# Block products of the output projection of batches 2 and 3: seven for eight

## The chip, the cores and the metric

The kernel runs on 1 core of one Trainium2 chip. The metric is the device time of one execution in microseconds (us); lower is better. The engines are TensorE (PE, matrix products into PSUM), VectorE (DVE), ScalarE (ACT), GpSimd (POOL) and SyncE (SP, which issues the DMAs).

## What is computed

```python
# attention: q, k, v of (4, 12, 448, 64), causal, float32
scores = np.where(mask, -1e9, (1 / np.sqrt(64)) * np.matmul(q, k.transpose(0, 1, 3, 2)))
attn = np.exp(scores - max); attn = attn / (sum + 1e-09)
attn_out = np.matmul(attn, v)
# tokens (1792 = 4 batches x 448) times weights (768 x 768), float32
x = attn_out.transpose(0, 2, 1, 3).reshape(1792, 768)
h = np.maximum(np.maximum(x @ w1, x @ w2), x @ w3)
out = h @ w_out
```

## The kernel before

Float32 values are split into two float16 planes, a high and a low one, so that one float32 product of a 128 x 128 weight block with a 128 x 448 token block is three matmuls on PE (high-high, high-low, low-high), each 448 columns wide. Everything is kept transposed: blocks of 128 features on the partitions, the 448 tokens of a batch along the free dimension. `w16[j]` holds the planes of w1, w2, w3 (j = 0 to 2) and of the output weights (j = 3).

Attention runs batch by batch (`staging`, `attend`), head pairs in turn, and fills x, whose low half is written on DVE (L532). For batches 0 and 1, `hidden` (L1022) makes six hidden blocks of 3 x 18 matmuls each, and `project` (L1315) the output: for each of six column blocks of the output weights 6 row blocks x 3 = 18 matmuls into one PSUM bank, an eviction with a scale (L512 on ACT, L514 on DVE) into `osb`, and a store (L1329, SP).

The hidden products of batches 2 and 3 are done together, by `seven` (L1246): x of the two batches, cut in two by features, is one 2 x 2 block matrix, w1 to w3 cut in two both ways is another, and seven products of combined blocks stand for the eight plain ones. For each of i = 0 to 2 (a 128-wide slice of both column halves) and j = 0 to 2 (the weight matrix), seven products of 9 matmuls each are summed up in five PSUM banks and folded together on DVE (L1259: read PSUM, scale, add; one fold after another in the same buffers e1, u3, c22). The maximum over j is taken on DVE (L1290), and the four hidden blocks of i are split in planes (high half L512 on ACT or L514 on DVE, low half L532 on DVE).

The combined operands are made ahead of it: `weights_combined` (groups S) rebuilds four float32 weight blocks from their planes (`load`, L1100, on DVE or POOL; a first sum at L1149), combines them (L1105, DVE) and splits four results in planes (high half L512 or L514, low half L532, 128 x 384), 16 instructions for each of the nine (i, j). `tokens_combined` (groups T) does the same for x (sums at L1179). All but the first S read `DONE`, that is, they wait until x of batch 3 is complete, since their buffers lie where attention's were. `columns` makes the per-column scale factors.

`project` of batches 2 and 3 takes the hidden blocks in pairs (z, z + 3), the pairs of the later i last, so that matmuls on the first hidden blocks can run while the last are being made.

The order of all work is written out: `ORDER` lists every instruction group in the order of issue over all engines, `ENGINE` names its engine. A POOL instruction is made to wait for the DVE instruction last ordered ahead of it that works from SBUF (`port=True`). PSUM has 8 banks; in this stage the ring M has 3 and L has 5. SBUF regions are used twice, first for attention and then for the late stage (`regions`). The kernel's matmuls of the late stage all have the same form:

```python
for wl, hl in ((0, 0), (0, 1), (1, 0)):
    PE.matmul(T(M)[:, 0:S_LEN], w16[3][:, f, wl, es], T(("h", b, f))[:, hl], start=..., stop=...)
```

## Time and profile before

| | |
|---|---|
| time, median of 3 runs | 468.86 us (468.77 to 470.32) |
| the profiled execution, its own time | 471.05 us |
| its span, first to last instruction | 469.3 us |
| PE busy | 460.2 us (98%), 3732 matmuls |
| DVE busy | 390.6 us (83%) |
| ACT busy | 309.3 us (66%) |
| POOL busy | 137.7 us (29%) |
| mean granted clock of PE | 0.996 of full speed |

Times in the rows are us from the start of the span unless marked ns. A group's row gives line, engine, operation, output <- input, shapes and count, then its busy time, the mean of one, and the idle time of the engine just ahead of them. L12 is line 12 of the kernel; a helper's line stands for all its callers.

### The profile page before, as it was taken

The numbers are of one execution on the slowest core, as the hardware profiler recorded it, in microseconds if no ns is written. First come the engines' busy times: TensorE is split into PE (matmuls) and PEld (weight loads), VectorE is DVE, ScalarE is ACT, GpSimd is POOL, SyncE is SP. The second block draws the span as 40 slices with busy tenths as digits, with TensorE's granted clock in tenths as the row PEclk, the third lists the DMA queues.
The fourth block names the chain that finished last, engine by engine and source line by source line (L and its number), as shares of the span: only waits on it lengthen the run. The fifth ranks groups of instructions, "written<-read, shape, count | busy, mean of one in ns | idle before, by whom it ended". The sixth has DMA issues, their size and how long they took to land.

```text
span 469.3 us, 9754 instructions
## 1 busy us (share of the span) xinstructions
PE 460.2 (98%) x3732; PEld 269.5 (57%) x3732; DVE 390.6 (83%) x750; ACT 309.3 (66%) x730; POOL 137.7 (29%) x164
## 2 busy tenths in 40 slices
PE   7999999999999999999999999999999999999996
PEld 4778765565665556565556556655555555555553
DVE  3899999999999998896568979888999988897510
ACT  4899999999999999876776788783422411211202
POOL 4024523461433334631265442301032130000000
PEclk9899999999999999999999999999999999999999
DMA  8856378998998877656757744762100000000122
GB/s 236 293 176 217 117 233 224 229 211 184 188 225 227 201 234 198 129 102 146 143 124 159 171 87 71 170 123 47 39 0 2 0 1 1 1 0 1 49 91 97
DMA packets 102319, 60.40 MB, mean 129 GB/s; under 512 B 76672, under 2 KB 99712, under 8 KB 102272
## 3 DMA queue, kind: packets, MB, share of 16 engines
q1 hardware_dynamic: 102272, 59.78, 51.2%
q8 instruction: 29, 0.48, 0.4%
q14 instruction: 18, 0.15, 0.1%
HBM read 35.39 MB, written 5.51 MB: 87 GB/s over the span
## 4 chain that ended last, share of the span: by engine, by line
PE 85%; DVE 7%; ACT 3%; DMA 2%; issue 1%; POOL 1%; SPq 1%; ACTq 0%; DVEq 0%; POOLq 0%
PE M L1022 24%; PE M L1315 15%; PE L L1246 12%; PE S L706 11%; PE M L1246 7%; PE O L820 6%; PE O L1246 4%; PE L L1315 2%; DMA region<-in_k_dram 2%; DVE acc L733 1%; DVE region L938 1%; DVE region L930 1%; DVE region L942 1%; ACT region L744 1%; PE M L551 1%
## 5 line engine op out<-in xcount | busy, mean ns | idle before, releaser
L1022 PE MATMUL M<-x,w 128*128 128x448 f16 x648 | 127.9, 353 | 0.2 <-POOL x L523 0.2
L1022 PEld LDWEIGHTS <-w 128*128 128x128 f16 x648 | 61.2, 98 | 58.1 <-issue 3.1
L744 ACT ACTIVATE region<-S,acc 128x384 f32<-128x384 f32 (+3 forms) x168 | 82.3, 503 | 8.5 <-DVE acc L733 5.6
L523 POOL TENSOR_TENSOR region<-region 128x1024 f16<-128x1024 f32 x23 | 49.0, 2132 | 80.9 <-ACT region L512 26.1
L733 DVE TENSOR_REDUCE acc<-S 128x2 f32<-128x512 f32 (+2 forms) x96 | 61.5, 682 | 12.0 <-PE S L706 10.3
L706 PE MATMUL S<-region 64*128 64x384 f32 (+4 forms) x384 | 66.6, 404 | 0.4 <-DMA region<-in_k_dram 0.4
L1315 PEld LDWEIGHTS <-w 128*128 128x128 f16 x432 | 41.4, 98 | 38.1
L1315 PE MATMUL M<-h,w 128*128 128x448 f16 x288 | 56.9, 353 | 0.0
L512 ACT ACTIVATE region<-region,acc 128x256 f32<-128x256 f32 (+3 forms) x94 | 45.4, 533 | 11.5 <-DVE acc L774 11.5
L706 PEld LDWEIGHTS S<-region 64*128 64x128 f32 (+1 forms) x384 | 40.6, 188 | 18.7 <-issue 11.2
L512 ACT ACTIVATE region<-region,cols 128x384 f16<-128x384 f32 (+1 forms) x31 | 18.3, 612 | 47.4 <-DVE region L1105 23.5
L1246 PEld LDWEIGHTS <-region 128*128 128x128 f16 x324 | 31.7, 98 | 29.6
L512 ACT ACTIVATE region<-region 128x1024 f16<-128x1024 f32 (+2 forms) x48 | 40.8, 863 | 9.1 <-DVE region L1179 3.9
L1100 POOL TENSOR_TENSOR region<-w 128x384 f32<-128x384 f16 x16 | 15.3, 968 | 72.8 <-DVE region L1100 27.1
L1246 PE MATMUL L<-region,region 128*128 128x448 f16 x180 | 36.3, 352 | 0.0
L1246 PEld LDWEIGHTS <-w 128*128 128x128 f16 x243 | 23.6, 98 | 22.0
L744 ACT ACTIVATION_READ_ACCUMULATOR region<-S,acc 128x1 f32 x168 | 34.7, 206 | 0.0
L1246 PE MATMUL M<-x,w 128*128 128x448 f16 x162 | 32.8, 353 | 0.0
L820 PEld LDWEIGHTS <-region 128*64 128x64 f16 x1080 | 26.7, 111 | 9.1 <-issue 8.2
L820 PE MATMUL O<-region,region 128*64 128x128 f16 (+1 forms) x1080 | 30.6, 211 | 0.1
L512 ACT ACTIVATE hacc<-M,cols 128x448 f32<-128x448 f32 x9 | 5.7, 631 | 30.5 <-PE M L1246 20.4
L532 DVE SCALAR_TENSOR_TENSOR w<-region,wf,w 128x768 f16<-128x768 f32 x20 | 20.5, 1038 | 4.6 <-POOL w L516 4.3
(152 smaller groups left out, 733.5 us busy)
## 6 DMA issues: line engine op xcount, KB each, us to landing
region<-in_moe_w_dram SPq DMA_DIRECT2D x18, 768.0 KB, 4.4
region<-in_q_dram SPq DMA_DIRECT2D x24, 224.0 KB, 3.4
region<-in_k_dram SPq DMA_DIRECT2D x24, 224.0 KB, 3.4
out_dram<-osb SPq DMA_DIRECT2D x24, 224.0 KB, 2.0
region<-in_v_dram SPq DMA_DIRECT2D x12, 384.0 KB, 5.9
region<-in_moe_w_out_dram SPq DMA_DIRECT2D x6, 768.0 KB, 4.4
region<-in_v_dram SPq DMA_DIRECT2D x4, 192.0 KB, 5.2
region<-region SPq DMA_TRANSPOSE x36, 4.6
```

Source lines behind the costliest of these rows:

```text
L512: ACT.activation(o, i, AF.Copy, scale=f)
L523: ENG[eng].tensor_tensor(out=o, in0=i, in1=hi, op=ALU.subtract)
L532: DVE.scalar_tensor_tensor(out=o, in0=i, scalar=f, in1=hi, op0=ALU.mult, op1=ALU.subtract)
L551: PE.matmul(T(M)[:, i * P : i * P + P], ap(c, 0, [[0, P]]), ident, start=True, stop=True)
L706: PE.matmul(o[:, c : c + w], l, r, start=start, stop=True, skip_group_check=True)
L733: DVE.tensor_reduce(out=T(acc)[:, at : at + len(g)], in_=i, op=ALU.max, axis=AX.XY if parts == 2 else AX.X, negate=True)
L744: ACT.activation(part(T(y), parts, c, w), part(T(S), parts, c, w), AF.Exp, bias=T(acc)[:, at : at + 1], accum_out=T(acc)[:, 7 + at : 8 + at])
L820: PE.matmul(T(O)[D * h : D * h + D, P * i : P * i + w], vt[j][:, vl, (2 * p + h) * D : (2 * p + h + 1) * D], T(pT[u])[:, 8 * pl + c, a : a ...
L1022: PE.matmul(T(M)[:, 0:S_LEN], w16[j][:, kk, wl, fs], xx[:, kk % 3, xl], start=(kk == 0 and wl + xl == 0), stop=(kk == 5 and wl == 1))
L1100: add(c_add(n), lambda e: ENG[e].tensor_tensor(out=o(), in0=a()[0], in1=a()[1], op=ALU.add), reads=reads, writes=writes, ring=ring, prio=p ...
L1246: PE.matmul(T(M)[:, 0:S_LEN], stat(c, wl), mov(c, xl), start=first and n == 0, stop=n == 8, skip_group_check=True)
L1315: PE.matmul(T(M)[:, 0:S_LEN], w16[3][:, f, wl, es], T(("h", b, f))[:, hl], start=(f == 0 and hl + wl == 0), stop=(f == 5 and wl == 1))
```

## The change

`project` is now used for batches 0 and 1 only. For batches 2 and 3, `project_seven` takes the hidden blocks of the two batches as one 2 x 2 block matrix (batch by feature half) and the output weights as another, and forms seven products of 9 matmuls for each of three column pairs, each issued in two parts (row blocks 0 and 1, then 2), in five PSUM banks, with two evictions, five folds on DVE and four stores. `weights_combined` is called for j = 3 too (three more sets of 16 instructions), with constants for scale factors. `heads_combined` makes the combined hidden blocks for each i: a difference, three scaled differences on DVE, and four splits in planes; one of the four plain hidden blocks of each i (12) is no longer split. The new planes have buffers of their own (`uA`, `uB`) in regions that are now used a third time, and in x of batch 3. `h3` shrinks from 6 to 3 buffers. `ORDER` (1865 entries before, 1958 after) and `ENGINE` are new throughout.

```diff
--- before
+++ after
@@ -32,129 +32,135 @@
-ORDER = [16, 15, 17, 18, 19, 20, 30, 21, 31, 32, 48, 49, 50, 0, 2, 3, 4, 1, 6, 5, 47, 22, 23, 24, 26, 27, 25, 28, 29,
...
@@ -167,7 +173,7 @@
...
-    tT=4, tS=6, tL=8, h3=6, Se=2, Sl=6, tE=3, L=5)
+    tT=4, tS=6, tL=8, h3=3, Se=2, Sl=6, tE=3, L=5, uA=2, uB=1)
...
@@ -426,12 +432,12 @@
...
-        Se=([P, DM], F32), Sl=([P, DM], F32))
+        Se=([P, DM], F32), Sl=([P, DM], F32), uA=([P, 3, 2, S_LEN], F16), uB=([P, 3, 2, S_LEN], F16))
-        (("p32", "ph", "pT"), ("Sl", "tS")), (("wst", "w3"), ("tT",)), (("vr",), ("Se", "tE")), (("v16",), ("tL",)),
-        (("qr", "kr"), ("h3",)))
+        (("p32", "ph", "pT"), ("Sl", "tS")), (("wst", "w3"), ("tT",)), (("vr",), ("Se", "tE"), ("uA",)), (("v16",), ("tL",)),
+        (("qr", "kr"), ("h3", "uB")))
...
@@ -496,6 +503,7 @@
+    pc = wmx
@@ -1088,8 +1096,15 @@
...
+        def heads(e):
+            rec(pc[:, 12:15], wg[:, 0:3])
+            tt(out=pc[:, 0:3], in0=wg[:, 3:6], in1=pc[:, 12:15], op=ALU.mult)
+            for k, f in ((3, 0.5), (6, 0.25), (9, -0.25)):
+                times(pc[:, k : k + 3], wg[:, 0:3], f)
+
+        add([("dve", 0.7)], heads, reads=["kap"], writes=["pc"], prio=prio, port=True)
@@ -1117,11 +1132,11 @@
...
-        od.group = f"S{3 * i + j}"
+        od.group = f"S{3 * i + j if j < 3 else 9 + i}"
-        kp, kn = kap[:, q : q + 1], kap[:, 9 + q : 10 + q]
+        kp, kn = (kap[:, q : q + 1], kap[:, 9 + q : 10 + q]) if j < 3 else (1.0, -1.0)
@@ -1140,7 +1155,8 @@
...
-            planes(lambda: at(0), lambda: at(1), lambda: g(name)().rearrange("p (a b) -> p a b", b=P), kpa[:, f + q : f + q + 1],
+            planes(lambda: at(0), lambda: at(1), lambda: g(name)().rearrange("p (a b) -> p a b", b=P),
+                   kpa[:, f + q : f + q + 1] if j < 3 else (0.25 if f else 0.5),
@@ -1248,7 +1264,7 @@
...
-                add([("pe", 9 * c_pe(S_LEN))], mm, reads=reads + (DONE if z != 1 else []), writes=[M], ring=ring, prio=pr + 0.01 * at,
+                add([("pe", 9 * c_pe(S_LEN))], mm, reads=reads + (DONE if z != 1 else []), writes=[M, ("pd", i, j, at)], ring=ring, prio=pr + 0.01 * at,
@@ -1291,7 +1307,7 @@
...
-        for z, b, f in ((11, 2, i), (12, 3, i), (22, 3, i + 3), (21, 2, i + 3)):
+        for z, b, f in ((11, 2, i), (22, 3, i + 3), (21, 2, i + 3)):
@@ -1300,6 +1316,116 @@
...
+
+    UN = [("x", 3, 0), ("uB", 0), ("uA", 0), ("uA", 1)]
+
+    def heads_combined(c, prio):
+
+        od.group = f"T{3 + c}"
+        o = {z: ("tL", "c", c, z) for z in (11, 12, 21, 22)}
+        one_, two = ("tL", "v", c), ("hacc", "v", c)
+        ratio = pc[:, c : c + 1]
+        seen = [(TT[z], k) for z in range(4) for k in range(3)] + [("pd", 0, 0, k) for k in range(7)]
+
+        def less(t, a, b, ring=None, reads=()):
+            add([("dve", c_sb(S_LEN))],
+                lambda e: DVE.scalar_tensor_tensor(
+                    out=T(t), in0=T(a), scalar=ratio, in1=T(b), op0=ALU.mult, op1=ALU.subtract),
+                reads=[a, b, "pc"] + list(reads), writes=[t], ring=ring, prio=prio, port=True)
+
+        def plane(z, t, k):
+            u, f = UN[z], pc[:, k + c : k + c + 1]
+            r = ("uB" if z == 1 else "uA", u) if z and c == 0 else None
+            add([("act", c_act(S_LEN, 0.06)), ("dve", c_dve(S_LEN, True) + 0.06)],
+                lambda e: scaled(e, T(u)[:, c, 0], T(t), f), reads=[t, "pc"] + seen + ([(u, "u", 0, 0)] if c else []),
+                writes=[(u, "u", c, 0)], ring=r, prio=prio, port=True)
+            add([("dve", c_sb(S_LEN))], lambda e: scaled_rest("dve", T(u)[:, c, 1], T(t), f, T(u)[:, c, 0]),
+                reads=[t, (u, "u", c, 0)], writes=[(u, "u", c)], prio=prio, port=True)
+
+        add(c_add(S_LEN), lambda e: ENG[e].tensor_tensor(out=T(one_), in0=T(o[12]), in1=T(o[11]), op=ALU.subtract),
+            reads=[o[12], o[11]], writes=[one_], ring=("tL", one_), prio=prio, port=True)
+        less(two, o[22], one_, ("hacc", two))
+        less(o[12], o[22], o[12])
+        plane(0, one_, 3)
+        plane(1, two, 6)
+        plane(2, o[12], 3)
+        less(o[21], o[21], two, reads=[(("h", 2, c + 3), 1)])
+        plane(3, o[21], 9)
+
+    def project_seven(prio):
+        f4, f16, m4 = (pc[:, 15 + z : 16 + z] for z in range(3))
+        f1 = osc[:, 2:3]
+        for ee in range(3):
+            od.group = f"j{12 + ee}"
+            s = [("Sw", ee, 3, z) for z in range(2)]
+            bank = {z: ("P", 3, ee, z) for z in (1, 4, 5, 6, 7)}
+            e1, u3, c11, c22 = (("tL", n, 3, ee) for n in ("e1", "u3", "c11", "c22"))
+            es = [slice((ee + 3 * z) * P, (ee + 3 * z + 1) * P) for z in range(2)]
+
+            def w(half, z, es=es):
+                return (lambda c, hl: w16[3][:, 3 * half + c, hl, es[z]]), lambda c: [("w", 18 + 3 * half + c)]
+
+            def sw(z, s=s):
+                def at(c, hl):
+                    return T(s[z // 2]).bitcast(F16).rearrange("p (s c h f) -> p s c h f", s=2, c=3, h=2)[:, z % 2, c, hl]
+
+                return at, lambda c: [(s[z // 2], z % 2, 0), (s[z // 2], z % 2)]
+
+            def hb(b, half):
+                return (lambda c, hl: T(("h", b, 3 * half + c))[:, hl]), lambda c: [(("h", b, 3 * half + c), z) for z in range(2)]
+
+            def ub(z):
+                return (lambda c, hl: T(UN[z])[:, c, hl]), lambda c: [(UN[z], "u", c, 0), (UN[z], "u", c)]
+
+            def product(z, stat, mov, first, at, bank=bank):
+                M = bank[z]
+                for part in ((0, 1), (2,)):
+
+                    def mm(e, part=part):
+                        for c in part:
+                            for wl, xl in ((0, 0), (0, 1), (1, 0)):
+                                PE.matmul(
+                                    T(M)[:, 0:S_LEN], stat[0](c, wl), mov[0](c, xl), start=first and c + wl + xl == 0,
+                                    stop=c == 2 and wl == 1, skip_group_check=True)
+
+                    claim = first and part[0] == 0
+                    add([("pe", 3 * len(part) * c_pe(S_LEN))], mm, reads=[n for c in part for n in stat[1](c) + mov[1](c)],
+                        writes=[M], ring=(("M" if z == 1 else "L"), M) if claim else None, prio=prio + 0.2 * ee + 0.01 * at,
+                        chain="L" if claim and z != 1 else None)
+
+            def evict(o, ring, bank=bank):
+                add([("act", c_act(S_LEN, 0.02)), ("dve", c_dve(S_LEN) + 0.06)],
+                    lambda e: scaled(e, T(o), T(bank[1])[:, 0:S_LEN], f1), reads=[bank[1], ("osc", 2)], writes=[o], ring=(ring, o),
+                    prio=EV)
+
+            def fold(o, z, f, a, reads, writes, ring=None, bank=bank):
+                add([("dve", c_dve(S_LEN) + 0.06)],
+                    lambda e: DVE.scalar_tensor_tensor(
+                        out=T(o), in0=T(bank[z])[:, 0:S_LEN], scalar=f, in1=T(a), op0=ALU.mult, op1=ALU.add),
+                    reads=[bank[z], ("osc", 2)] + reads, writes=writes, ring=ring, prio=EV)
+
+            def store(o, z, b, es=es):
+                add(c_dma((P, 4 * S_LEN)), lambda e: ENG[e].dma_start(out[es[z], b * S_LEN : (b + 1) * S_LEN], T(o)), reads=[o],
+                    prio=EV)
+
+            product(1, w(0, 0), hb(2, 0), True, 0)
+            evict(e1, "hacc")
+            product(6, sw(2), ub(1), True, 1)
+            fold(e1, 6, f16, e1, [], [e1])
+            product(1, w(1, 0), hb(2, 1), False, 2)
+            evict(c11, "osb")
+            store(c11, 0, 2)
+            product(7, sw(1), ub(2), True, 3)
+            fold(u3, 7, f4, e1, [e1], [u3], ("tL", u3))
+            product(5, sw(0), ub(0), True, 4)
+            fold(c22, 5, f4, u3, [u3], [c22], ("tL", c22))
+            store(c22, 1, 3)
+            product(4, w(1, 1), ub(3), True, 5)
+            fold(u3, 4, m4, u3, [], [u3])
+            store(u3, 1, 2)
+            product(5, sw(3), hb(3, 1), False, 6)
+            fold(e1, 5, f4, e1, [], [e1])
+            store(e1, 0, 3)
 
     def project(b, prio):
         for e2 in range(KC):
@@ -1345,16 +1471,27 @@
                     if i + j:
                         weights_combined(i, j, 400 + 10 * (3 * i + j))
             for i in range(3):
+                weights_combined(i, 3, 500 + 10 * i)
+            for i in range(3):
                 seven(i, prio + 0.1 + 0.2 * i)
+                heads_combined(i, prio + 0.2 + 0.2 * i)
+        else:
+            return
 
         od.group = "k"
 
         def factor(e):
             DVE.tensor_scalar(
                 out=osc[:, b : b + 1], in0=bsc[:, b, 9:10] if b < 2 else bsc[:, 2, 8:9], scalar1=wu[:, 6:7], scalar2=2.0**18, op0=ALU.mult, op1=ALU.mult)
-
-        add([("dve", 0.13)], factor, reads=[("scale", b) if b < 2 else "beta", "wu"], writes=[("osc", b)], prio=prio)
-        project(b, prio)
+            if b == 2:
+                for z, f in enumerate((4.0, 16.0, -4.0)):
+                    DVE.tensor_scalar(out=pc[:, 15 + z : 16 + z], in0=osc[:, 2:3], scalar1=f, scalar2=None, op0=ALU.mult)
+
+        add([("dve", 0.13 if b < 2 else 0.5)], factor, reads=[("scale", b) if b < 2 else "beta", "wu"], writes=[("osc", b)], prio=prio)
+        if b < 2:
+            project(b, prio)
+        else:
+            project_seven(prio + 1)
 
 
     DVE.memset(junk, 0.0)
```

## Rows read from the trace of the kernel before

**Rows 1.** The page, part 1: busy time, share of the span, instructions.

```profile
PE 460.2 (98%) x3732; PEld 269.5 (57%) x3732; DVE 390.6 (83%) x750; ACT 309.3 (66%) x730; POOL 137.7 (29%) x164
```

**Rows 2.** Stretches: busy us (instructions) by engine, granted clock, DMA share, GB/s.

```profile
core 0: us, PE busy (x) PEld busy (x) DVE busy (x) ACT busy (x) POOL busy (x), PEclk, DMA share, GB/s
0.00:326.00 326.00, 320.61 (x2996) 197.53 (x2997) 284.19 (x567) 277.15 (x676) 121.78 (x147) 0.99 0.72 175
...
331.20:441.85 110.65, 110.65 (x587) 57.24 (x585) 99.52 (x174) 23.94 (x41) 15.41 (x17) 1.00 0.00 1
441.85:469.30 27.45, 23.69 (x126) 12.04 (x123) 1.96 (x3) 5.07 (x8) 0.00 (x0) 1.00 0.27 101
```

**Rows 3.** End of the chain that ended last: start, us, engine, tile, line, count.

```profile
446.25 19.31 PE M L1315 x102
465.63 0.63 ACT osb L512
```

**Rows 4.** Whom DVE waited for, 326 to 441.85: us, times, longest.

```profile
DVE region L532 <- ACT region L512: 3.0, 3, 1.6
DVE hacc L1259 <- PE L L1246: 2.1, 1, 2.1
DVE region L1259 <- PE L L1246: 1.0, 1, 1.0
DVE h L532 <- ACT h L512: 0.7, 1, 0.7
```

**Rows 5.** The same stretch, DVE's busy time and instructions.

```profile
326.00:441.85 115.85, 104.48 (x181) 1.00 0.01 5
```

**Rows 6.** DVE's groups in that stretch, shapes apart: busy us, mean ns, idle before.

```profile
L532 DVE SCALAR_TENSOR_TENSOR region<-region,cols 128x384 f16<-128x384 f32 x32 | 18.4, 614 | 2.5 <-ACT region L512 2.3
L1105 DVE SCALAR_TENSOR_TENSOR region<-region,cols 128x384 f32<-128x384 f32 x24 | 14.8, 615 | 0.6
L1259 DVE SCALAR_TENSOR_TENSOR region<-L,cols,region 128x448 f32<-128x448 f32 x14 | 9.5, 682 | 1.9 <-PE L L1246 1.0
L1100 DVE TENSOR_TENSOR region<-w 128x384 f32<-128x384 f16 x17 | 8.8, 551 | 0.1
...
L532 DVE SCALAR_TENSOR_TENSOR region<-region,cols,region 128x448 f16<-128x448 f32 x6 | 4.1, 684 | 0.9 <-ACT region L512 0.7
...
L514 DVE TENSOR_SCALAR region<-region,cols 128x384 f16<-128x384 f32 x5 | 3.1, 611 | 0.1
...
L514 DVE TENSOR_SCALAR region<-region,cols 128x448 f16<-128x448 f32 x5 | 2.3, 453 | 0.2
...
L1353 DVE TENSOR_SCALAR osc<-bsc,wu 128x1 f32<-128x1 f32 x1 | 0.2, 207 | 0.0
```

**Rows 7.** DVE in order of time: start, us, line, operation, count of adjoining instructions.

```profile
332.75 1.49 DVE L1100 TENSOR_TENSOR region<-w 128x384 f32<-128x384 f16 x3
...
336.93 2.20 DVE L532 SCALAR_TENSOR_TENSOR region<-region,cols 128x384 f16<-128x384 f32 x4
...
343.34 1.92 DVE L1105 SCALAR_TENSOR_TENSOR region<-region,cols 128x384 f32<-128x384 f32 x3
...
391.88 0.61 DVE L1105 SCALAR_TENSOR_TENSOR region<-region,cols 128x384 f32<-128x384 f32 x1
```

**Rows 8.** POOL's pair and DVE beside it in time; durations of DVE's line 1290.

```profile
358.14 1.78 POOL L1100 TENSOR_TENSOR region<-w 128x384 f32<-128x384 f16 x2 [5.19 <-DVE region L532]
...
359.36 1.04 DVE L1290 TENSOR_TENSOR region<-region 128x448 f32<-128x448 f32 x1
...
L1290 DVE TENSOR_TENSOR region<-region x12: 614/619/1036, 352.8 to 440.0; 128x448 f32<-128x448 f32 x12
```

**Rows 9.** Early stretches: PE busy and granted clock among the columns of rows 2.

```profile
5.00:10.00 5.00, 3.74 (x23) 2.10 (x21) 2.50 (x4) 1.47 (x5) 2.37 (x4) 1.00 1.03 329
10.00:15.00 5.00, 4.12 (x22) 2.94 (x23) 3.93 (x9) 3.80 (x15) 0.00 (x0) 0.77 1.08 317
20.00:25.00 5.00, 5.00 (x60) 4.27 (x55) 4.66 (x9) 4.97 (x16) 0.00 (x0) 1.00 0.36 119
```

More of the change, by code (lines that the diff above doesn't have):

```diff
@@ L139 @@
[L139 to L140 removed]
+    "acacposppepeacdvspsppoacpedvdvacacacacacdvacacacacacdvsppedvdvacacacacdvacacacacposppepeacdvspsppopopedvdvacacac"
+    "acacdvacacacacacdvsppedvdvacacacacdvacacacacposppepeacdvspsppopopedvdvacacacacacdvacacacacacposppedvdvacacacacdv"
+    "acacacacposppepeacdvspacspacspacspacdvpedvdvdvdvacdvacdvacpoacdvspacspacspacspacdvpedvdvdvdvpopoacdvacdvpodvdvsp"
@@ new lines @@
+    "sppopopedvdvacacacacacdvdvacacacacposppedvdvacacacacdvacacacacposppepedvdvspsppopopedvdvacacacacacdvdvacacacacpo"
+    "sppedvdvacacacacdvacacacacposppepeacdvspsppoacpedvdvacacacacacdvdvacdvacdvdvsppedvdvacacacacdvdvacacacdvsppepeac"
+    "dvspsppoacpedvdvacacacacacdvacdvacacdvdvsppedvdvacacacacdvacacdvdvdvsppepedvdvspsppopopedvdvacacacacacdvdvdvacac"
+    "dvdvsppedvdvacacacacdvacdvacacposppepedvdvspsppoacpedvdvacacacacacdvdvdvacacdvdvsppedvdvacacacacdvdvacacacposppe"
+    "peacdvspsppopopedvdvacacacacacdvdvacdvacdvposppedvdvacacacacdvdvdvdvdvposppepedvdvspsppopopedvdvacacacacacdvacac"
@@ L141 @@
+    "acacacposppedvdvacacacacdvacdvacdvdvsppepeacdvspsppopopedvdvacacacacacdvdvacacdvdvposppedvdvacacacacdvdvacacacpo"
+    "sppepeacdvspsppopopedvdvacacacacacdvdvacdvdvacposppedvdvacacacacdvacacacdvdvsppepedvdvspsppoacpedvdvacacacacacdv"
+    "dvdvacdvdvdvsppedvdvacacacacdvdvacacacposppepeacdvspsppoacpedvdvacacacacacdvacacdvdvacdvsppedvdvacacacacdvdvdvac"
     "acdvsppepeacdvspacdvdvdvdvspacdvdvdvdvspacdvdvdvdvpedvdvdvdvdvdvpopopodvacdvspacdvdvdvdvspacdvdvdvdvspacdvdvdvdv"
@@ L153 @@
[L153 to L157 removed]
+    "spacdvdvdvdvspacdvdvdvdvpedvdvdvdvdvdvacpoacdvacdvspacdvdvdvdvspacdvdvdvdvspacdvdvdvdvpedvdvdvdvdvacdvacdvacdvsp"
@@ new lines @@
+    "acdvdvdvdvspacdvdvdvdvspacdvdvdvdvpedvdvdvdvdvpodvpopodvdvdvacacacacacacpepepeacpepepedvpepepedvacpopepepeacpepe"
+    "pedvpepepedvacpopepepeacpepepedvpepepedvacpopepepeacpepepedvpepepedvacdvpepepeacpepepedvpepepedvacpopepepeacpepe"
+    "pedvpepepedvacdvdvpepepeacsppepepeacsppepepedvsppepepeacsppepepedvsppepepedvsppepepeacpepepedvpepepedvacpopepepe"
+    "acpepepedvpepepedvacdvpepepeacpepepedvpepepedvacdvpepepeacpepepedvpepepedvacpopepepeacpepepedvpepepedvacpopepepe"
+    "acpepepedvpepepedvacpodvpepepeacsppepepeacsppepepeacsppepepeacsppepepeacsppepepeacspdvdvdvpopodvdvdvacdvacdvdvdv"
@@ new lines @@
+    "dvdvacdvdvdvdvdvdvdvacdvacdvdvdvacdvacdvdvpodvdvdvdvacdvacdvdvdvacdvacdvdvpopodvdvdvacdvacdvdvdvacdvacdvdvdvdvdv"
+    "dvdvacdvacdvdvdvacdvacdvdvpodvpodvdvacdvacdvpodvacdvacdvdvpopodvdvdvacdvacdvdvdvacdvacdvpopopodvdvdvacdvacdvpodv"
+    "acdvacdvpopodvdvdvdvacdvacdvpodvacdvacdvpodvdvdvdvdvacdvacdvdvdvacdvacdvdvdvpopodvdvacdvacdvdvdvacdvacdvdvdvpodv"
+    "dvdvacdvacdvpodvacdvacdvpopopopodvdvacdvacdvdvdvacdvacdvpopopopodvdvacdvacdvpodvacdvacdvpopopopodvdvacdvdvdvpodv"
+    "acdvacdvpeacpedvpedvpedvpedvpepedvdvpeacpedvpedvpedvpedvpepedvdvdvdvdvpeacpedvpedvpedvpedvpepedvdvdvdvdvacdvacdv"
@@ L159 @@
+    "acdvpodvdvacdvacdvacdvdvacdvpeacpedvpeacpedvpedvpepedvdvpeacpedvpedvpedvpedvpepedvdvdvdvdvpeacpedvpedvpedvpedvpe"
+    "pedvdvdvdvdvacdvacdvacdvpodvdvacdvacdvacdvdvacdvpeacpedvpeacpedvpedvpepedvdvpeacpedvpedvpedvpedvpepedvdvdvdvdvpe"
+    "acpedvpedvpedvpedvpepedvdvdvdvdvacdvacdvacdvdvdvdvacdvacdvacdvdvacdvdvpepeacpepedvpepedvsppepedvpepedvsppepedvsp"
+    "pepedvsppepeacpepedvpepeacsppepedvpepedvsppepedvsppepedvsppepeacpepedvpepeacsppepedvpepedvsppepedvsppepedvsp")
 PLAIN = 6
@@ L459, in attention_moe @@
     buf = {}
-    for n, (early, then) in enumerate(regions):
-        size = [sum(RINGS[r] * words(*kinds[r]) for r in part) for part, kinds in ((early, shapes), (then, late))]
-        assert size[1] <= size[0], (early, size)
+    for n, lives in enumerate(regions):
+        kinds = [late if z else shapes for z in range(len(lives))]
+        size = [sum(RINGS[r] * words(*kind[r]) for r in part) for part, kind in zip(lives, kinds)]
+        assert max(size) == size[0], (lives, size)
         region = c1.tile([P, size[0]], F32, name=f"region{n}")
-        carve(region, early, shapes)
-        carve(region, then, late)
+        for part, kind in zip(lives, kinds):
+            carve(region, part, kind)
     for r, (sh, t) in shapes.items():
```

30 lines of the change are left out of this document (3 added, 27 removed), and 179 rows, old and new, of the table ORDER.

## The prediction

> **What bounds the kernel now.** I read the page's busy shares first [rows 1], then the span cut at the points where VectorE's (DVE's) work changes [rows 2], then the end of the chain [rows 3], then what DVE waits for [rows 4]. TensorE (PE) is busy 460.2 of 469.3 us [rows 1]. All its idle time lies ahead of 326 us (5.4 us, the start-up and attention) and in the last 3.8 us; from 331 to the last matmul there is none [rows 2]. The chain ends in 102 matmuls on end, 19.31 us, then one eviction on ScalarE (ACT), then 3.04 us for the last store [rows 3]. So a matmul taken out of the last 140 us is worth its whole step, 19.31 / 102 = 0.189 us, if nothing else comes late.
>
> The candidate for being late stands in the same table. Between 331.2 and 441.85 us DVE is busy 99.5 of 110.65 us, and in the last 27 us only 2 [rows 2]. ACT is busy 24 of those 110, GpSimd (POOL) 15. DVE's last addition to the attention output (the low half of batch 3's x) starts at 326.0; from there to 441.85 DVE runs 181 instructions, 104.5 us busy and 11.4 idle [rows 5]. Of the idle time some 4 us wait for PE (DVE was ahead) and some 4 for ACT, 3.1 and 3.7 of it in the four longest entries [rows 4]; the rest is small gaps. Today these 27 us of empty DVE at the end are the reserve.
>
> **The change, part by part.**
>
> *PE.* Two projections of 6 column blocks x 6 row blocks x 3 plane pairs = 108 matmuls each (216) become 3 column pairs x 7 products x 9 = 189. Widths are unchanged (448 columns), so 27 x 0.189 = 5.1 us go, all of it in the stretch where PE never idles. Nothing is added on PE.
>
> *Where the new work can run.* The order table leaves the last attention products where they were: summing the PE steps ahead of them in both tables gives the same place within 0.3 us, and the first product of combined operands stands 1.7 us earlier. So the S and T sums, for which batch 3 must be finished, cannot start sooner, and I count DVE's instructions from the low half of batch 3's last x on in both tables: 181 before (184 with three late evictions) and 227 after.
>
> *DVE's balance.* By kind, from the ENGINE table, each at its group's busy time per instruction [rows 6]: low halves of 384 wide, 12 more x 0.575 = 6.9; multiply-adds of 384, 9 x 0.617 = 5.6; reads of weight pairs, one more net (3 more first sums, 2 fewer second ones), 0.5; high halves of 384, 4 fewer (now ACT) x 0.62 = -2.5; low halves of 448, 12 new less 3, 9 x 0.68 = 6.1; sums of hidden blocks, 9 x 0.68 and one plain, 6.7; high halves of 448, 6 fewer (ACT) x 0.46 = -2.8; evictions of the new products, 16 less one first-column eviction, 15 x 0.68 = 10.2; five instructions on a few columns, 5 x 0.2 = 1.0. Together +31.7. The groups' busy times overlap at their seams (all 25 add up to 110.8 where the engine shows 104.5), so times 0.943: +29.9. DVE then has 104.5 + 29.9 = 134.4 us of work.
>
> *What it has to fit into.* With PE gapless, the last matmul ends at 465.56 - 5.1 = 460.5, and the last instruction is now a fold on DVE (0.68) in place of an ACT eviction (0.63): it ends at 461.2. From 326.0 that is 135.2 us. DVE must be busy 134.4 of 135.2; before, it idled a tenth. That is the whole question, so I bound DVE's demand from both sides.
>
> High end: idle in the same proportion to busy as before, without the waits for PE, (115.85 - 4) / 104.5 = 1.07: 143.8 us, 8.6 beyond what there is. Low end: the idle time vanishes and pairs get shorter. Two adjoining DVE instructions where the second reads the first cost more than independent ones: four independent low halves take 2.20, a step of 0.53; three chained multiply-adds take 1.92, a step of 0.65 [rows 7]. Counting in the tables adjoining instructions of which one reads the other's output, I find 63 among 184 before and 45 among 227 after; at the old share there would be 78. 33 fewer x 0.13 = 4.3: 130 us, no stall at all. Value taken: DVE's densest stretch, 332.75 to 391.88 [rows 7], where it was nearly the bound: 99 instructions in 59.1 us with one wait for PE of 1 us [rows 4], so 0.588 each without it, and 29 chained pairs. 227 x 0.588 = 133.5; the mean of the new mix is 0.592 busy against 0.577, x 1.026 = 136.9; 22 fewer chained pairs than at that stretch's share, -2.9: 134.0; waits, since the folds follow PE's pace and half the low halves follow ACT, 3 (below the 8 of before, since a DVE that is behind finds its operands ready): 137.0. That is 1.8 us beyond the 135.2, and PE waits that long, in several pieces.
>
> *ACT and POOL.* ACT's instructions in this stretch go from 54 to 82; 28 x 0.62 = 17 us more on an engine busy 24 of 110: hidden while its high halves are issued in time. POOL goes from 17 to 33 additions, 0.89 each and more [rows 8], 31 us of 135: hidden in itself. One row shows what it can cost DVE: POOL's pair of additions runs from 358.14 to 359.92, and a DVE maximum that started at 359.36 took 1.04 us where the median of its line is 0.62 [rows 8]. That is 0.42 lost of 0.56 shared. The Trainium skill (SBUF — State Buffer, Who interferes with whom) says that a DVE instruction with two SBUF inputs contends with POOL's reads and that the loser is held for the other's whole instruction; by that all 15.4 us of POOL's new additions could be taken from DVE, and the sum would be 468.86 - 5.1 + 15.4, some 479. In the tables each POOL addition stands beside DVE's reads of PSUM, which in the rows keep their 0.68 us there: the folds beside POOL's 31.1 us last 34.7, and 1.0 us is uncovered (0.7 of 15.7 before). The 0.3 between is inside the 1.8.
>
> *Buffers, stores, wait queues.* The extra planes live in regions whose former tenants (the first S set, the q and k stages, x of batch 3) are done 30 us or more earlier by the table: nothing waits. Stores stay 12, on SP, the last one 3.04 us long as before: no change. The new products accumulate in 5 PSUM banks per column pair, and M1 takes its second half only after ACT has evicted its first; behind that eviction in ACT's queue stand only high halves. What is late next is the last hidden column: its last fold, maximum, three differences, high and low halves stand as ten DVE instructions in the table, 6.2 us, and two thirds of the first column pair's products, which need the first two hidden columns alone, are put ahead of the first product that needs the third: 9.7 us of PE after the last hidden product. With that cover the chain costs nothing; without it 6 us would lie bare.
>
> *Sum.* 469.3 - 5.1 + 1.8 + 0.05 = 466.05 us span. The profiled execution lasted 471.05, 1.75 around its span; the median of the runs shown is 468.86, 2.2 below it. Applied to the median: 468.86 - 3.2 = 465.6.
>
> **Rivals.**
> 1. *PE stays gapless.* DVE needs 135 us or less, as its low end allows; for it speak the fewer chained pairs, against it that no stretch of before shows DVE at 99%. 468.86 - 5.1 = 463.8.
> 2. *DVE takes over as the bound, partly.* Waits as large as before (8 us in place of 3) or a dense rate without the saving by pairs: stall 3 to 7, so 466.8 to 470.8. For it: the waits for ACT in 390 to 437 us exist today [rows 4]; the new low halves each follow an ACT high half.
> 3. *DVE takes over wholly, and the kernel is slower.* Mechanism: the idle share of before stays, 143.8 us of DVE time from 326 on, 8.6 of stall: 468.86 - 5.1 + 8.6 = 472.4. It decides from the point where the stall passes the 5.1 us saved (DVE demand over 140.3). POOL would do the same if DVE lost to its 15.4 new us what that one maximum lost, 0.42 of 0.56: 11.6.
> 4. *The clock.* PE idled 2.1 us within 5 to 15 us, and 10 to 15 shows a granted clock of 0.77 [rows 9], a mix of 2.4 and 1.2 GHz: 46% of 5 us at the lower level, 1.15 us lost; from 20 us on it is 1.00 again [rows 9]. If the stalls bunch up so late in the kernel, one such fall: 465.6 + 1.2 = 466.8. Against it: small pieces.
> 5. *It doesn't do what it says*, that is, the searched table also moves attention's 5.4 us of PE idle [rows 2]: 1 us either way, 464.6 to 466.6.
>
> **How the numbers follow.** A change under 0.5% (2.3 us, so 466.5 to 471.2) cannot be told from none here. Forecast with rival 5 around it 0.45; rival 1 0.19; rivals 2 and 4 0.28; rival 3 0.08. Faster by over 0.5%: the forecast's and rival 1's chance less a little of the edge, 0.63; within: 0.30; slower: 0.07. The range runs from just under rival 1 to the middle of rival 2: 463.5 to 469.2, which leaves out rival 3 and the upper part of rival 2, under 0.2.
>
> **What would show it.** PE: 27 matmuls fewer, 0.189 us steps; idle of 1 to 3 us between 380 and 455 us, put down to DVE (low halves, folds). DVE: 132 to 138 us from its last x to its last instruction, over 95% busy, no longer empty in the last 20 us. If PE's idle there is nil, rival 1; over 5, rival 3. Wrong altogether would be a DVE that is done by 440 us (then I miscounted what was added), or a fall of the granted clock after 100 us.

## The result and the profile after

| | before | after |
|---|---|---|
| median, runs taken side by side (6 each) | 469.94 us | 464.70 us |
| ratio, 95% interval | | 0.9894 [0.9874, 0.9914] |
| profiled span | 469.3 us | 463.1 us |
| matmuls | 3732 | 3705 |

The change saves 1.06%, some 5.0 us. In the changed kernel the line numbers have moved: the folds of `seven` are L1275, its products L1262, the low halves L540, the high halves L520 (ACT) and L522 (DVE), the combinations L1120, the loads L1115, the maxima L1306; `project_seven` has its products in L1387 and its folds in L1403.

The page, part 1, answers to [rows 1]; from part 2, DVE's line (busy tenths of 40 slices of 11.6 us):

```profile
PE 453.9 (98%) x3705; PEld 266.1 (57%) x3705; DVE 415.0 (90%) x801; ACT 323.2 (70%) x760; POOL 149.2 (32%) x177
...
DVE  3899999999999999996787789889999999999984
```

Stretches with the columns of [rows 2]: up to the last attention products, the late stage, and the end. Then DVE alone from its last low half of x on, with the columns of [rows 5]:

```profile
0.00:326.00 326.00, 320.61 (x3002) 197.41 (x3003) 288.34 (x574) 276.85 (x679) 118.68 (x144) 0.99 0.72 175
326.00:440.00 114.00, 114.00 (x604) 58.93 (x603) 111.31 (x202) 43.49 (x77) 26.29 (x29) 1.00 0.01 5
440.00:463.10 23.10, 19.28 (x102) 9.78 (x100) 15.40 (x27) 2.89 (x6) 4.26 (x5) 0.97 0.32 120
...
323.68:460.00 136.32, 128.85 (x231) 1.00 0.06 23
```

PE is busy for all of the 114 us, and from there up to the end of its last matmul at 459.28 us. DVE, which idled a tenth of the late stage before [rows 2], is busy 111.3 of the 114 us (98%), and PE still never waits for it.

The end of the chain [rows 3], and whom DVE waited for from 323.6 us on [rows 4]:

```profile
450.20 9.09 PE L L1387 x48
459.29 0.02 issue
459.32 0.68 DVE hacc L1403
...
DVE region L1403 <- PE L L1387: 2.0, 2, 1.0
DVE hacc L1403 <- PE L L1387: 1.0, 1, 1.0
DVE region L540 <- ACT region L520: 0.6, 1, 0.6
DVE region L1403 <- PE O L1387: 0.4, 1, 0.4
```

Before, the longest entries were 3.7 us for ACT and 3.1 for PE. Now 3.4 of some 4.6 us are for PE, in the last folds, where DVE has caught up. PE sets the end, as before: the span ends with matmuls on end, one fold on DVE, and the last store.

DVE's dearest groups from 323.6 us on, shapes apart [rows 6]:

```profile
L540 DVE SCALAR_TENSOR_TENSOR region<-region,cols 128x384 f16<-128x384 f32 x32 | 18.5, 612 | 0.0
L1120 DVE SCALAR_TENSOR_TENSOR region<-region,cols 128x384 f32<-128x384 f32 x24 | 14.7, 614 | 0.5
...
L540 DVE SCALAR_TENSOR_TENSOR region<-region 128x384 f16<-128x384 f32 x12 | 6.2, 551 | 0.6 <-ACT region L520 0.6
L1120 DVE SCALAR_TENSOR_TENSOR region<-region 128x384 f32<-128x384 f32 x9 | 5.0, 554 | 0.2 <-POOL region L1165 0.2
```

The last two rows are the new sets of the output weights: same operation, same shape, but the factor is a constant of the instruction and not a column of `cols`, and one takes 0.55 us for 0.61.

### The profile page after: what moved, and what is told of

It reads as the page before. It is cut to its first block, busy times and chain, and to the rows that moved or that the text cites. A ratio compares the mean times of both kernels' runs of the same rounds, so it can differ in the third digit from the quotient of the medians.

```text
span 463.1 us, 9807 instructions
## 1 busy us (share of the span) xinstructions
PE 453.9 (98%) x3705; PEld 266.1 (57%) x3705; DVE 415.0 (90%) x801; ACT 323.2 (70%) x760; POOL 149.2 (32%) x177
## 4 chain that ended last, share of the span: by engine, by line
PE 84%; ACT 9%; DMA 2%; DVE 2%; issue 1%; DVEq 0%; ACTq 0%
PE M L1030 25%; PE L L1262 14%; PE S L714 11%; PE M L1441 9%; PE M L1262 7%; PE O L828 6%; PE L L1387 4%; ACT region L752 4%; PE O L1262 3%; ACT region L520 3%; DMA region<-in_moe_w_dram 2%; PE M L1387 2%; ACT region L953 1%; PE O L1387 1%; PE M L559 1%
## 5 line engine op out<-in xcount | busy, mean ns | idle before, releaser
L1030 PEld LDWEIGHTS <-w 128*128 128x128 f16 x648 | 61.3, 98 | 57.8 <-issue 2.3
L752 ACT ACTIVATE region<-S,acc 128x128 f32<-128x128 f32 (+3 forms) x168 | 82.4, 504 | 10.9 <-DVE acc L741 8.2
L520 ACT ACTIVATE region<-region 128x1024 f16<-128x1024 f32 (+3 forms) x58 | 44.6, 777 | 18.5 <-DVE region L1195 6.9
L520 ACT ACTIVATE region<-region,acc 128x384 f32<-128x384 f32 (+3 forms) x93 | 44.3, 530 | 12.1 <-DVE acc L782 12.1
L520 ACT ACTIVATE region<-region,cols 128x384 f16<-128x384 f32 (+1 forms) x38 | 22.9, 615 | 37.7 <-DVE region L1120 25.7
L1262 PEld LDWEIGHTS <-region 128*128 128x128 f16 x324 | 31.7, 98 | 29.6
L1115 POOL TENSOR_TENSOR region<-w 128x384 f32<-128x384 f16 x25 | 22.3, 913 | 79.3 <-DVE region L540 26.8
L1441 PE MATMUL M<-h,w 128*128 128x448 f16 x216 | 42.8, 353 | 0.0
L1262 PE MATMUL L<-region,region 128*128 128x448 f16 x207 | 41.3, 353 | 0.0
L1262 PEld LDWEIGHTS <-w 128*128 128x128 f16 x243 | 23.5, 98 | 21.8
L1262 PE MATMUL M<-x,w 128*128 128x448 f16 x162 | 32.8, 353 | 0.0
L1441 PEld LDWEIGHTS <-w 128*128 128x128 f16 x216 | 20.4, 98 | 19.5 <-issue 1.0
L938 DVE TENSOR_SCALAR_CACHE_REDUCE region<-region 128x768 f32<-128x768 f32 x24 | 22.3, 940 | 1.1 <-ACT region L953 1.0
L950 DVE SCALAR_TENSOR_TENSOR region<-region 128x768 int32<-128x768 int32 x24 | 22.8, 955 | 0.3
```

Of the source, the lines that this page charges most:

```text
L520: ACT.activation(o, i, AF.Copy, scale=f)
L752: ACT.activation(part(T(y), parts, c, w), part(T(S), parts, c, w), AF.Exp, bias=T(acc)[:, at : at + 1], accum_out=T(acc)[:, 7 + at : 8 + at])
L938: DVE.tensor_scalar(out=T(x32), in0=T(x32), scalar1=MIN_HI, scalar2=None, op0=ALU.max, op1=ALU.max, accum_out=wmx[:, c])
L950: DVE.scalar_tensor_tensor(out=xi(), in0=word(1), scalar=TOP2, in1=xi(), op0=ALU.bitwise_and, op1=ALU.bitwise_or)
L1030: PE.matmul(T(M)[:, 0:S_LEN], w16[j][:, kk, wl, fs], xx[:, kk % 3, xl], start=(kk == 0 and wl + xl == 0), stop=(kk == 5 and wl == 1))
L1262: PE.matmul(T(M)[:, 0:S_LEN], stat(c, wl), mov(c, xl), start=first and n == 0, stop=n == 8, skip_group_check=True)
```

## The experiments

Two plain copies of the changed kernel were run beside experiments, on the same chips. What was expected of the first: 

> The changed kernel as it is, as the measure for the three others on the same chip. 0.989 of the kernel before, within 0.003.

 It took 464.22 us, 0.9885 of before [0.9853, 0.9917]. Of the second: 

> The changed kernel unchanged, on the same chip as the two beside it: 464.2 us, 0.9885 of the kernel before, within 0.3%.

 It took 464.86 us, 0.9891 [0.9862, 0.9920]. Where an experiment has no copy beside it, differences below are taken from 0.989 of before, the mean of these two and of the first comparison, times 469.5 us.

**Does PE pace the end of the changed kernel?** The 27 matmuls are put back in `project_seven`:

```diff
+                        if z == 7 and part[0] == 0:
+                            for c in (0, 1, 0):
+                                for wl, xl in ((0, 0), (0, 1), (1, 0)):
+                                    PE.matmul(T(M)[:, 0:S_LEN], stat[0](c, wl), mov[0](c, xl), ...)
```

> The changed kernel with its 27 saved matmuls put back: in each of the three column pairs of the output projection the product M7 runs nine more matmuls of the same shape ahead of its own, which start the bank afresh, so nothing else moves. If PE paces the end in the changed kernel too (theory A: PE has no idle from 326 us on in its trace), each costs its step of 0.189 us and the time rises by 5.1 us, to about that of the kernel before. If DVE, 97% busy there, paces it (theory B), PE's extra work disappears in its waits for DVE: 0 to 2 us.

Measured: 470.83 us, 1.0018 [0.9986, 1.0051], 6.0 us more than the changed kernel. Its late stage is gapless too:

```profile
326.00:440.00 114.00, 114.00 (x604) 59.00 (x603) 111.16 (x202) 42.91 (x75) 26.09 (x28) 1.00 0.01 5
```

From the first product of the late stage (at 327.51 us here, at 326.32 in the changed kernel) to the end of the last matmul its trace shows 138.07 us, the changed kernel's 132.96: 5.11 = 27 x 0.189. PE is the bound, to the matmul.

**What are 27 matmuls worth without the new work?** In the kernel before, matmuls are left out, first spread over the projections of batches 2 and 3 (the low weight plane), then at the end (the low hidden plane); nothing is added on DVE. Both edits were meant to leave out 27, and the expectations say so, but neither does. The function that issues the matmuls is called when the loop over the column blocks is over, so that `e2` is 5 in every one of these tests. The first edit leaves out 24 (3708 matmuls in its trace for 3732), the second 36, the low hidden plane in all six column blocks of batch 2 (3696).

```diff
+                            if b > 1 and wl == 1 and (f in (1, 4) or f == 3 and e2 % 2 == 0 and b == 2):
+                                continue
```

> The kernel before with 27 matmuls left out of the two output projections (the products of the weights' low plane with two of six hidden blocks in batches 2 and 3, and three more; the output lacks them), and nothing else changed: PE's share of the change without any of DVE's 30 us of new work. Theory A: 5.1 us faster than before, and the same as the changed kernel within 1 us, since there the new work of DVE costs nothing. Theory B (DVE's new work costs PE some stalls that the trace hides in matmul ends, and the new order table gives something back elsewhere): this one is faster than the changed kernel by more than 1 us.

```diff
+                            if hl and ((b, e2) in ((2, 0), (2, 5), (3, 2), (2, 2)) or (b, e2) == (2, 3) and f in (0, 3, 1)):
+                                continue
```

> The kernel before with 27 matmuls left out once more, now all in the last five column blocks of the output projections, where no other engine's work is hidden behind them (the products of the weights' high plane with the low plane of the hidden blocks; the output lacks them). If the run with 27 left out between the hidden products fell short of 5.1 us because they were cover for DVE and ACT there (its trace shows 0.6 us of new waits of PE after 326 us), this one gains the full 5.1 us, 0.989 of the kernel before, and equals the changed kernel within 1 us. If the changed kernel owes part of its gain to its new order table, this one stays at the 0.994 of the other run.

Measured: spread 465.92 us, 0.9941 [0.9917, 0.9966], that is 2.8 us for the 4.5 of 24 steps; at the end 463.82 us, 0.9863 [0.9830, 0.9897], that is 6.4 us for the 6.8 of 36 steps. PE's late stretch with the spread cut, and two of the places where it now waits, then the one place in the run with the cut at the end (start, duration, count, and in brackets the idle time ahead and its releaser):

```profile
326.00:440.00 114.00, 113.38 (x599) 58.38 (x597) 103.41 (x180) 27.07 (x46) 15.68 (x18) 1.00 0.01 5
...
411.82 1.86 PE L1246 MATMUL M<-x,w 128*128 128x448 f16 x9 [0.29 <-ACT hacc L512]
422.88 1.86 PE L1246 MATMUL L<-region,w 128*128 128x448 f16 x9 [0.27 <-DVE hacc L1259]
```

```profile
441.57 0.54 PE L1317 MATMUL L<-region,w 128*128 128x448 f16 x2 [0.37 <-DVE region L532]
```

From the first product of the late stage to the end of the last matmul the three traces show 138.06 us (before), 134.64 (spread) and 131.95 (at the end). The spread cut thus gives 3.42 us, 1.12 less than 24 steps, and the cut at the end 6.11, 0.70 less than 36. Counting each product from the start of the one ahead, three products of the first run start late, by 0.45, 0.23 and 0.44 us, and one of the second, by 0.70: the whole shortfall of both traces. A projection put between two products is also their cover: shortened, it lets PE reach a bank that ACT or DVE has not yet freed, or a hidden block that DVE has not yet split.

That the second run comes near the changed kernel is therefore not the equality that its expectation had in mind, since it has 9 matmuls less. With 9 x 0.189 = 1.7 us put back, a kernel with 27 fewer and no new work would take 465.5 us; the changed kernel, with some 24 us more of DVE work, takes 464.2 beside it, and the intervals of the two runs leave some 2 us open. The traces are finer: 131.95 + 1.70, less the one late start of 0.70, is 132.95 us, and the changed kernel shows 132.96. The new work on DVE, ACT and POOL costs nothing that can be measured.

**Does the new order table move the head of the kernel?** The kernel before with the first 1030 entries of the new order and its engines:

```diff
-ORDER = [16, 15, 17, 18, 19, 20, 30, 21, 31, 32, 48, 49, 50, 0, 2, 3, 4, 1, 6, 5, 47, ...
+ORDER = [16, 17, 15, 18, 19, 48, 49, 20, 21, 0, 1, 47, 30, 31, 32, 2, 3, 4, 6, 5, 7, ...
```

> The kernel before with the first 1030 entries of the changed kernel's order table and their engines (loads, values, the first heads of attention, the first hidden blocks: some 215 us), and the rest in its own order. If the new table brings something of its own ahead of the late stage, which the changed kernel's trace hints at (its last matmul ends 6.3 us sooner, 1.2 more than 27 matmuls), this is 1 us faster than the kernel before, 0.9975. If the 1.2 us are the ordinary variation between executions: 1.000 within 0.002.

Measured: 470.37 us, 1.0012 [0.9989, 1.0035]. These 1030 entries, some 215 us of the kernel, bring no gain above 0.5 us. For the stretch from there to 326 us there is no run, but PE is busy 320.61 us of the first 326 in the trace before [rows 2] and in the one after. The profiled spans differ by 6.2 us, 1.1 more than the matmuls account for; the same first product of the late stage starts at 326.32, 327.20 and 325.74 us in three executions of the changed kernel, so an offset of that size is a matter of single executions.

**How much does DVE have in hand?** One more multiply-add of 128 x 384 in each of the 12 weight sets (into a buffer that nobody reads), then two in each:

```diff
+                DVE.scalar_tensor_tensor(out=junk, in0=more(), scalar=f, in1=mk16, op0=ALU.mult, op1=ALU.subtract)
...
-        combine(g(12), g(12), kp, g(11), ["kap", t[11]], [t[12]], n, prio)
+        combine(g(12), g(12), kp, g(11), ["kap", t[11]], [t[12]], n, prio, more=g(11))
```

> The changed kernel with one more DVE instruction (128x384, float32 times factor minus float16, written to an unused tile) behind the last multiply-add of each of the 12 sets of combined weights: 11 of them from 326 us on, 0.55 to 0.61 us each, 6.5 us of DVE in the stretch where it is 97% busy. Theory A with a small reserve of DVE of 2 to 3 us: PE now waits, and the time rises by 3.5 to 4.5 us. Theory C (DVE's busy share overstates its load, the reserve is over 6 us): under 1 us. Theory D (no reserve at all): the whole 6.5 us.

> As the run with 12 more DVE instructions, with two in each set: 22 of them from 326 us on, 13 us of DVE. Theory A with a reserve of 2 to 3 us: 10 to 11 us more than the changed kernel, so that the step from 12 to 24 costs its full 6.5 us. Theory C: well below that, 5 us or less.

Measured: 468.41 us, 0.9981 [0.9961, 1.0000], and 474.95 us, 1.0124 [1.0096, 1.0153]. The busy lines of the first and the second, and PE's stretch in each:

```profile
PE 455.1 (97%) x3705; PEld 265.9 (57%) x3705; DVE 421.8 (90%) x813; ACT 323.8 (69%) x760; POOL 149.5 (32%) x177
326.00:440.00 114.00, 111.61 (x587) 57.26 (x586) 111.53 (x203) 41.53 (x72) 26.04 (x28) 1.00 0.01 5
```

```profile
PE 455.9 (96%) x3705; PEld 266.3 (56%) x3705; DVE 428.5 (91%) x825; ACT 323.9 (69%) x760; POOL 149.5 (32%) x177
326.00:440.00 114.00, 107.61 (x562) 54.76 (x561) 111.63 (x205) 38.87 (x67) 26.06 (x28) 1.00 0.01 5
...
387.83 3.56 PE L1267 MATMUL L<-region,region 128*128 128x448 f16 x18 [1.20 <-DVE hacc L1280]
398.02 1.86 PE L1267 MATMUL L<-x,region 128*128 128x448 f16 x9 [1.52 <-DVE region L1280]
```

DVE's busy time over the whole kernel rises by 6.8 and 13.4 us, but the first weight set is made before the late stage. From DVE's last low half of x on, 11 and 22 of the added instructions run, and DVE is busy 128.85 us in the changed kernel, and 134.22 and 139.87 us in these two (columns of [rows 5]): 5.4 and 11.0 us more.

```profile
324.31:490.00 165.69, 134.22 (x242) 1.00 0.06 20
```

```profile
324.06:490.00 165.94, 139.87 (x253) 0.99 0.06 20
```

The time rises by 4.3 and 11.0 us, each uncertain by more than 1 us. In the traces the stretch from the first product to the last matmul grows by 4.07 and 9.35 us. So by the traces 1.3 and 1.7 us were in hand, by the times no more than that, and beyond it the full price is paid: between the two runs 5.65 us more on DVE make the stretch 5.28 us longer. Rivals 2 and 3 of the prediction were thus a few microseconds away.

**Do chained neighbours cost DVE what the prediction took?** The changed kernel with 29 entries of its order moved, by which 155 stand at another place, so that 72 of DVE's neighbours in the late stage read what stands just ahead of them, for 42:

```diff
-... 1500, 1501, 1502, 1504, 1505, 1503, 1508, ...
+... 1500, 1501, 1502, 1503, 1504, 1505, 1508, ...
```

> The changed kernel with DVE's instructions reordered so that more of them stand right behind the one whose output they read: 72 adjoining pairs of this kind from 326 us on in place of 42, by moving single instructions a few places, everything else in order. If chained pairs cost DVE 0.13 us each, as the rows of before suggest, DVE needs 3.9 us more and, with the reserve of 2.6 to 3 us that the runs with 12 and 24 more instructions show, the time rises by 1 to 2 us, a little more where a moved instruction keeps ACT waiting. If the pairs cost nothing (DVE hides the dependence): no change, under 0.5 us.

Measured: 470.65 us, 1.0029 [1.0008, 1.0050], 6.8 us more; the expectation was far too low. DVE's stretch, first of the unchanged order on the same chip, then of this one:

```profile
323.60:470.00 146.40, 129.66 (x233) 0.99 0.06 23
```

```profile
323.60:470.00 146.40, 133.00 (x233) 0.99 0.06 23
...
357.75 0.99 DVE L1214 TENSOR_TENSOR region<-region,hacc 128x448 f32<-128x448 f32 x1
364.93 1.13 DVE L1214 TENSOR_TENSOR region<-region 128x448 f32<-128x448 f32 x1
...
373.64 1.86 PE L1170 MATMUL M<-x,w 128*128 128x448 f16 x9 [1.78 <-ACT hacc L428]
386.79 3.56 PE L1170 MATMUL L<-region,region 128*128 128x448 f16 x18 [1.07 <-DVE hacc L1183]
```

DVE is 3.3 us longer busy for 30 more chained pairs. But 1.4 of it are single instructions grown longer (the groups' own times add up to 142.8 us for 141.4), such as the two maxima of 0.99 and 1.13 us for 0.62, which is what [rows 8] showed beside POOL (the unchanged order has one such, of 1.08); the other 1.9 us are seams that no longer overlap, 0.06 us a pair for the 0.13 I had taken. The rest of the 6.8 us is order: PE waits 4.6 us in five places, 3.4 of them for evictions on ACT. The longest, 1.78 us, ends on ACT like this (columns as in PE's rows above):

```profile
372.46 0.61 ACT L428 ACTIVATE region<-region,cols 128x384 f16<-128x384 f32 x1 [0.51 <-DVE region L1028]
372.98 0.61 ACT L428 ACTIVATE hacc<-M,cols 128x448 f32<-128x448 f32 x1
```

The eviction that PE needs stands in ACT's queue behind a high half which waits for DVE. A pair's price and a shifted due time can't be separated in this run.

**Is it the constant factor that makes the new sums short?** The four constants are read from columns in SBUF:

```diff
-        kp, kn = (kap[:, q : q + 1], kap[:, 9 + q : 10 + q]) if j < 3 else (1.0, -1.0)
+        kp, kn = (kap[:, q : q + 1], kap[:, 9 + q : 10 + q]) if j < 3 else (pc[:, 18:19], pc[:, 19:20])
...
-                   kpa[:, f + q : f + q + 1] if j < 3 else (0.25 if f else 0.5),
+                   kpa[:, f + q : f + q + 1] if j < 3 else (pc[:, 21:22] if f else pc[:, 20:21]),
```

> The changed kernel, with the constants 1, -1, 0.5 and 0.25 of the unscaled sums of the output weights read from four columns in SBUF instead of being held in the instructions: the same arithmetic, the same order, four tiny instructions more on VectorE. Theory D (a factor that is held in the instruction makes a 128x384 sum on VectorE shorter, 0.55 us for 0.61 us): the 12 and 9 sums that took 0.551 and 0.554 us rise to 0.61, VectorE's busy time after 323 us grows by 1.3 us and its four columns by some 0.3; with 2.6 us in hand (the two runs with added sums) TensorE still does not wait, and the time is 464.2 to 465 us. Rival (the shorter sums are shorter for their place beside other work, not for their operands): they stay at 0.55 us and the busy time does not move.

Measured: 464.61 us, 0.9896 [0.9862, 0.9930], no change. The two groups:

```profile
L540 DVE SCALAR_TENSOR_TENSOR region<-region,wmx 128x384 f16<-128x384 f32 x12 | 6.9, 613 | 0.7 <-ACT region L520 0.7
...
L1122 DVE SCALAR_TENSOR_TENSOR region<-region,wmx 128x384 f32<-128x384 f32 x9 | 5.5, 613 | 0.6 <-POOL region L1167 0.5
```

It is the operand: 0.613 us for 0.551 and 0.554, whatever stands beside them. DVE's stretch grows from 128.4 to 129.9 us and its reserve takes it up.

**What keeps POOL's additions from slowing DVE in the late stage?** Each POOL instruction waits for the DVE instruction last ordered ahead of it that works from SBUF. This wait is taken away in the whole kernel, then only behind the last attention product:

```diff
-    PORT_FROM = 0.0
+    PORT_FROM = 1e9
```

> The changed kernel without the waits that hold each of GpSimd's operations behind VectorE's last instruction that has both inputs in SBUF; the waits that the data ask for stay. Theory E (GpSimd's 34 operations in the last part, 31 us, slow VectorE only where an instruction with two SBUF inputs meets them, by the 0.4 us of the one pair seen before): a dozen more meetings at 0.4 us each make VectorE's busy time some 3 to 7 us longer, past the 2.6 us in hand, and the time is 465 to 469 us. Rival (the two engines do not disturb one another, the waits are needless): VectorE's busy time and the time stay within 0.5 us of the changed kernel's, or GpSimd's earlier ends make it a little faster.

```diff
-            if e == "pool" and last is not None and s >= self.PORT_FROM:
+            if e == "pool" and last is not None and s < 325.0:
```

> The changed kernel with GpSimd's waits for VectorE kept up to the last attention product and left out behind it, where the 34 operations of GpSimd for the combined operands stand. In the run without any of these waits 7.3 us of TensorE's loss lay ahead of 323.6 us and some 10 behind it. Theory E (there each meeting of GpSimd with an instruction of two SBUF inputs costs VectorE some 0.74 us; a dozen are 9 us, less the 2.6 us in hand): the time is 469 to 475 us, so the whole gain of the change is gone with the order of GpSimd's additions alone. Rival (the loss of that run came from its delayed first part, and the last part only followed): the time stays within 2 us of the changed kernel's 464.7.

Measured: 481.86 us, 1.0251 [1.0217, 1.0286], and 475.57 us, 1.0135 [1.0111, 1.0159]: 16.9 and 11.5 us more than the changed kernel, the first far beyond what I expected. The busy line of the first:

```profile
PE 457.4 (95%) x3705; PEld 266.4 (55%) x3705; DVE 439.7 (91%) x801; ACT 323.4 (67%) x760; POOL 166.5 (35%) x177
```

DVE and POOL do the same work in 24.8 and 18.1 us more than in the unchanged copy (414.9 and 148.4). One place of the second run, four neighbouring low halves on DVE and the two additions that POOL now runs beside them; then the same four in the changed kernel:

```profile
342.31 3.60 DVE L540 SCALAR_TENSOR_TENSOR region<-region,cols 128x384 f16<-128x384 f32 x4
...
343.01 1.22 POOL L1115 TENSOR_TENSOR region<-w 128x384 f32<-128x384 f16 x1 [5.51 <-DVE region L540]
344.30 1.19 POOL L1165 TENSOR_TENSOR region<-region 128x384 f32<-128x384 f32 x1
```

```profile
341.77 2.20 DVE L540 SCALAR_TENSOR_TENSOR region<-region,cols 128x384 f16<-128x384 f32 x4
```

Two meetings cost DVE 1.40 us, 0.70 each, and POOL 0.2 to 0.3 each. The waits do not prevent every meeting. One is left in the changed kernel, ahead of the late stage (POOL first, then DVE):

```profile
286.85 2.13 POOL L531 TENSOR_TENSOR region<-region 128x1024 f16<-128x1024 f32 x1 [0.96 <-ACT region L520]
...
287.03 2.43 DVE L1115 TENSOR_TENSOR region<-x 128x448 f32<-128x448 f16 x1
```

DVE's sum, which takes 0.63 us elsewhere, starts 0.18 us behind POOL's addition and ends 0.48 us after it: it is held for nearly the whole of it and loses 1.8 us. In the two runs with added work it is the added multiply-add that stands there, and it takes 2.48 us. The folds, which read one operand from PSUM, keep their 0.68 us (675 to 680 ns in both runs). In the second run DVE is 138.3 us busy from 323.6 us on for 128.4 in the unchanged copy, and PE waits 7.5 us. Its largest wait has a price of its own (first PE's step with the idle time ahead of it in brackets, then the stretch with the columns of [rows 2]):

```profile
449.96 3.31 PE L1387 MATMUL O<-region,region 128*128 128x448 f16 x9 [2.22 <-DVE hacc L1403]
...
450.00:453.40 3.40, 3.40 (x10) 1.33 (x10) 2.05 (x4) 0.21 (x1) 0.00 (x0) 0.53 0.49 180
```

## Why the prediction was right, and where it was not

The forecast was 465.6 us from a before of 468.86, a gain of 3.2; the measured gain is 5.0. The time lies inside the range, and the sign was right, but the case that came true is rival 1, PE gapless, which I gave 0.19. That the time is missed by only 0.9 us and the gain by 1.8 is luck: the before that I started from lies 1.1 us below that of the runs side by side. By rival 1's own sum, before less 5.1, the 469.94 us of the runs taken side by side become 464.8; 464.7 was measured.

*PE's term: right.* 27 x 0.189 = 5.1 us. The run with the matmuls put back shows 5.11 in its trace. The run that leaves 36 out at the end of the kernel before shows 6.11 and one late start of 0.70, together 36 steps.

*DVE's demand: the term that was mis-sized.* I took 137.0 us and hence a stall of 1.8. From its last low half of x to its last instruction DVE now takes 136.3 us with 3.4 of waits for PE in the last folds: a demand of some 132.9, and a stall of nil. (Of the 3.4 us, the runs with added work show that DVE could use only 1.3 to 1.7.) The demand was thus set some 4 us too high. Three sizes made the difference. The groups' own times were to be 110.8 + 31.7 = 142.5 us and are 140.6; 21 x 0.06 = 1.3 of these 1.9 us are the constant factors, which I costed at the 0.61 us of sums with a factor per column, and the run with columns shows that the operand is the cause. The overlap at the seams I took at the old 0.943; it is 128.85 / 140.6 = 0.916, worth 3.8 us. That there are fewer chained neighbours (42 to 45 in 227) I had seen, and credited with 2.9 us on another route, the dense stretch; the reordered run gives 0.06 us for one more pair where I took 0.13, so the better overlap is not settled as an effect of chains alone. Against these stand idle gaps that are not waits for PE: 4.0 us for the 3 I took.

*Where DVE starts: a miss in its favour that cost no time.* I held the start at 326.0 us; its last low half of x starts at 323.68. The run with the new head shows that the head alone changes no time.

*The budget: right.* I said 135.2 us; it is 136.3 by the earlier start and the same end relative to PE. DVE's 98% in the late stage is what the step "that is the whole question" asked about; "no stretch of before shows DVE at 99%" was no argument against it, since before DVE idled for PE and ACT too [rows 4].

*Rivals 2 and 3: not come true, but near.* Added DVE work shows 1.3 to 1.7 us in hand by the traces, then a full price per microsecond. Rival 3's form through POOL is real: with POOL free to run beside DVE the changed kernel takes 475.6 us, slower than before. It loses 11.5 us, near the 11.6 that I had worked out for that rival from one maximum's 0.42 us, but that the two agree is luck: DVE is busy 9.9 us longer, PE waits 7.5 us, and the clock told of below adds some 1.5. The Trainium skill (SBUF — State Buffer, Who interferes with whom) states that a DVE instruction with two SBUF inputs contends with POOL's reads and that the loser is held for the other's whole instruction. These runs agree that the two contend and that folds from PSUM do not. The hold at 287 us is as stated, nearly the whole of an addition of 2.13 us; in the four low halves it is 0.70 us beside additions of 1.2. My reading that the order keeps POOL beside the folds was right for the late stage, and the wait that does it is worth more than twice the gain of the change.

*Rival 4, the clock: did not occur in the changed kernel* (granted 1.00 from 326 us to its last matmul). It exists: behind the wait of 2.22 us above, PE's granted clock was 0.53 for 3.4 us, nearly the lower level of 1.2 GHz, and nine matmuls took 3.31 us for 1.86. In the run without any of POOL's waits an equal wait of 2.22 us at 459 us was followed by 1.00.

*Rival 5, attention's idle time: not seen.* PE idles 5.39 us ahead of 326 us in both traces.

*The last hidden column: covered, as said.* In the changed kernel PE has no gap between its last hidden product and its last matmul.
